# The first tile of the first expert taken from the first nine row tiles

## The chip, the cores and the metric

The kernel runs on one core of a Trainium2 chip. The metric is the device time of one execution in microseconds. The engines are PE (TensorE, matmul), PEld (its weight load), DVE (VectorE), ACT (ScalarE), POOL (GpSimd) and SP (SyncE, which only issues transfers here).

## The reference

Linear attention in eight batches feeds a mixture of eight experts that takes one expert for each token.

```python
def _attn_ref(q, k, v, g_norm):                  # (8, 8, 576, 64)
    kv = np.einsum('bhsd,bhse->bhde', k, v)
    out = np.einsum('bhsd,bhde->bhse', q, kv)
    rms = np.sqrt(np.mean(out * out, axis=-1, keepdims=True) + 1e-06)
    return (out / rms * g_norm).astype(np.float32)

def _moe_ref(x, w_gate, w_output_gate, w1, w2):  # x (4608, 512), 8 experts, F 1024
    logits = x @ w_gate
    e_idx = np.argmax(logits, axis=1)
    ...                                          # gate_w: softmax at e_idx; eom: sigmoid(x @ w_output_gate)
    for e in range(E):
        mask = e_idx == e
        h = np.maximum(x[mask] @ w1[e], 0.0)
        out[mask] = gate_w[mask, None] * eom[mask, e, None] * (h @ w2[e])
```

## The kernel before

The 4608 tokens are 36 row tiles of 128. The attention of a batch is a set of products kvps (line 563, loads kvm and rem), a transpose kvTps (581), a product with the gates mps (593), and for each row tile a product ops (642) with its evictions on ACT. The rows go to DRAM (xs, written by SP, line 1031), 16 columns of norms and scales for each row to the tables xr and xt. Row tiles are routed in four groups of 9, 7, 10 and 10 (GR). The first two groups, 16 tiles, are "early": from their rows each expert's first two tiles of 128 tokens (TA = 2) are made, so that the experts can start while the attention of the last four batches goes on. `route` is the routing of a group, in pieces: norms on DVE, the argmax, ranks by products rps (853 to 862), one-hot tiles la on DVE, ACT and POOL, a table of indices by products tblps (973). The table of the second group, the "lead", gives the indices gidx; `gather` (284) then has POOL fetch both tiles of expert 0, rows xg and norms tl each, by indirect transfers (279), and sets `issue_mark` (993), behind which SP sends the last chunk of w1.

All engines follow the order in which the code is written. `early` writes the attention of the first four batches and both routings; `late` is a generator of pieces of the later attention and routing, named `rest`, of which `early` takes four (PIECES) and `run` one behind each block of an expert. Where PE would stand idle, `constants` (531) puts products of a constant tile (cps) into its order; COLD holds their numbers.

Behind `early`, each of the two tiles is scaled by its norms on DVE (313), transposed on PE (tps, 343), split into a high and a low part (xT, by ACT 346 and DVE 347), and multiplied for f = 0 and 1 by `mm1_part` (369) in 128 columns. Weights are split likewise into whi and wlo (`split_hi`, `split_lo`, `split`). `run(0)` goes on with f = 2 to 7 over 256 columns (`mm1`, 387), with hT evicted by ACT (395) and DVE (397), and then the second layer yps (`mm2`, 423). The chunks of w2 go out on SP behind the scaling of tile 1 (a dependency in the main part). `xfree` is a pool of eight slots for kvm, qT and rows.

## Time and profile before

| | us |
|---|---|
| median of 3 runs | 585.74 (585.55 to 585.89) |
| the profiled execution: time, span | 581.15, 579.3 |
| PE busy | 555.1 (96%) |
| DVE busy | 345.7 (60%) |
| ACT busy | 285.4 (49%) |
| POOL busy | 221.2 (38%) |

The profile is of one execution. The span is what the trace shows from the first to the last instruction; the execution's own time is 1.85 us more, and the median of the runs another 4.6 us. All places below are in us from the span's start.

### The profile page before, as it was taken

How to read it: one execution, taken by the hardware profiler on the slowest of the kernel's cores; microseconds unless marked ns; L12 is line 12 of the kernel's file. 1: busy time of each engine (PE TensorE's matmuls, PEld its weight loads, DVE VectorE, ACT ScalarE, POOL GpSimd, SP SyncE). 2: the span in 40 equal slices, each digit the busy share in tenths (PEclk: the TensorE clock that was granted, in tenths of full speed). 3: DMA queues.
4: the chain of work that ended last, by engine and by line, in shares of the span. 5: the costliest groups of instructions: out<-in, count | busy, mean ns of one | idle time of the engine just before them, and what ended most of it. 6: DMA issues, size and time to landing. Idle time of an engine off the chain costs nothing.

```text
span 579.3 us, 11842 instructions
## 1 busy us (share of the span) xinstructions
PE 555.1 (96%) x4626; PEld 475.4 (82%) x4626; DVE 345.7 (60%) x634; ACT 285.4 (49%) x482; POOL 221.2 (38%) x203
## 2 busy tenths in 40 slices
PE   7998879999999999999999999999999999999995
PEld 3775668888888787988989889889897988888894
DVE  2268576565596989767586646436355463646450
ACT  1354356576567546656464434435354444535430
POOL 3342344432313252543565326235264543545202
PEclk9999999999999999999999999999999999999999
DMA  8999899797866574776855345346454645556201
GB/s 306 407 410 340 257 406 405 275 369 279 299 232 210 176 270 155 247 232 206 285 199 175 124 149 166 109 156 205 151 183 141 205 154 161 171 170 207 75 6 38
DMA packets 38586, 126.18 MB, mean 218 GB/s; under 512 B 6877, under 2 KB 8142, under 8 KB 38528
## 3 DMA queue, kind: packets, MB, share of 16 engines
q1 hardware_dynamic: 29520, 105.19, 52.4%
q0 software_dynamic: 8288, 19.82, 10.3%
q8 instruction: 38, 0.62, 0.4%
q10 hardware_dynamic: 720, 0.38, 0.2%
q14 instruction: 20, 0.16, 0.1%
HBM read 106.01 MB, written 19.91 MB: 217 GB/s over the span
## 4 chain that ended last, share of the span: by engine, by line
PE 78%; DVE 10%; DMA 5%; issue 3%; ACT 3%; POOL 1%; POOLq 0%; ACTq 0%; DVEq 0%; SPq 0%
PE hps L387 33%; PE yps L423 31%; PE ops L642 4%; PE tps L343 3%; PE kvps L563 3%; PE yps L417 3%; DVE wlo L263 2%; DMA ld<-kvm 1%; DMA wgs<-wg 1%; DMA wraw<-w 1%; ACT whi L260 1%; DVE wlo L256 1%; PE cps L538 1%; DVE hT L397 1%; DVE la L895 1%
## 5 line engine op out<-in xcount | busy, mean ns | idle before, releaser
L387 PE MATMUL hps<-xT,whi 128*128 128x256 f32 (+8 forms) x1008 | 218.0, 308 | 5.8 <-DVE hT L397 3.7
L423 PE MATMUL yps<-whi,hT 128*128 128x512 f32 (+3 forms) x592 | 199.0, 400 | 0.0
L387 PEld LDWEIGHTS hps<-xT,whi 128*128 128x128 f32 x1008 | 166.5, 190 | 12.4 <-DVE hT L397 5.2
L387 PE MATMUL hps<-xT,wlo 128*128 128x256 f32 (+8 forms) x504 | 153.2, 304 | 0.0
L423 PEld LDWEIGHTS yps<-whi,hT 128*128 128x128 f32 (+3 forms) x592 | 110.2, 186 | 24.0
L423 PE MATMUL yps<-wlo,hT 128*128 128x512 f32 (+3 forms) x296 | 116.1, 392 | 0.0
L436 POOL DMA_INDIRECT out<-y,oidx x42 | 48.7, 1160 | 173.7 <-ACT y L435 145.1
L395 ACT ACTIVATE hT<-hps 128x256 fp32r<-128x256 f32 (+8 forms) x128 | 54.9, 429 | 121.8 <-PE hps L387 116.6
L397 DVE SCALAR_TENSOR_TENSOR hT<-hps,hT 128x256 fp32r<-128x256 f32 (+9 forms) x168 | 62.9, 395 | 86.0 <-ACT hT L395 85.6
L256 DVE SCALAR_TENSOR_TENSOR wlo<-wraw,gcol,whi 128x1024 fp32r<-128x1024 f32 x62 | 84.0, 1356 | 43.5 <-ACT whi L253 41.4
L263 DVE TENSOR_TENSOR wlo<-wraw,whi 128x1024 fp32r<-128x1024 f32 x64 | 85.2, 1331 | 26.7 <-ACT whi L260 25.7
L387 PEld LDWEIGHTS hps<-xT,wlo 128*128 128x128 f32 x504 | 95.6, 190 | 0.3
L253 ACT ACTIVATE whi<-wraw,gcol 128x1024 fp32r<-128x1024 f32 x62 | 71.3, 1150 | 0.6 <-DVE wlo L263 0.6
L279 POOL DMA_INDIRECT xg<-xs,gidx x42 | 47.2, 1123 | 55.6 <-PE hps L387 36.4
L260 ACT CAST whi<-wraw 128x1024 fp32r<-128x1024 f32 x64 | 66.6, 1040 | 1.1 <-DMA wraw<-w 1.1
L279 POOL DMA_INDIRECT tl<-xt,gidx x42 | 55.3, 1316 | 28.6 <-PE hps L387 21.1
L313 POOL TENSOR_TENSOR xg<-xg,tl 128x512 f32<-128x512 f32 (+8 forms) x40 | 44.0, 1101 | 53.7 <-DMA tl<-xt,gidx 44.4
L423 PEld LDWEIGHTS yps<-wlo,hT 128*128 128x128 f32 (+3 forms) x296 | 55.3, 187 | 10.4
L435 ACT ACTIVATE y<-yps,tl 128x512 f32<-128x512 f32 (+3 forms) x37 | 25.4, 686 | 56.1 <-PE yps L423 44.1
L346 ACT CAST xT<-tps 128x512 fp32r<-128x512 f32 (+8 forms) x42 | 22.9, 546 | 41.6 <-PE tps L343 40.5
L347 DVE TENSOR_TENSOR xT<-tps,xT 128x512 fp32r<-128x512 f32 (+8 forms) x42 | 26.6, 636 | 19.5 <-ACT xT L346 19.3
L642 PE MATMUL ops<-aug,ld 64*64 64x80 f32 (+1 forms) x960 | 32.2, 244 | 1.4 <-ACT gp L673 1.3
(176 smaller groups left out, 431.2 us busy)
## 6 DMA issues: line engine op xcount, KB each, us to landing
wraw<-w SPq DMA_DIRECT2D x128, 512.0 KB, 4.6
ld<-kvm SPq DMA_DIRECT2D x32, 512.0 KB, 10.0
ld<-qT SPq DMA_DIRECT2D x18, 512.0 KB, 8.9
xs<-xrow SPq DMA_DIRECT2D x18, 512.0 KB, 4.9
ld<-rem SPq DMA_DIRECT2D x4, 512.0 KB, 5.8
xg<-xs,gidx POOLq DMA_INDIRECT x42, 4.3
tl<-xt,gidx POOLq DMA_INDIRECT x42, 4.7
out<-y,oidx POOLq DMA_INDIRECT x42, 3.3
```

Of the source, the lines that this page charges most:

```text
L253: he.activation(hi, r, AF.Copy, scale=gcol[:, 0:1])
L256: eng.scalar_tensor_tensor(out=lo, in0=r, scalar=gcol[:, 0:1], in1=hi.bitcast(F32), op0=ALU.mult, op1=ALU.subtract)
L260: he.copy(hi, r)
L263: eng.tensor_tensor(out=lo, in0=r, in1=hi.bitcast(F32), op=ALU.subtract)
L279: return nc.gpsimd.indirect_dma_start(out=o[:M, :], out_offset=None, in_=dram[0:XE] if i < E else dram, in_offset=bass.IndirectOffsetOnAxi ...
L313: return eng.tensor_tensor(out=v, in0=v, in1=f, op=ALU.mult)
L387: seq.append(nc.tensor.matmul(ps[:, :C], w[:, o:o + P], x[d][:, :C], start=(d == 0 and k == 0), stop=(d == 3 and k == 2)))
L395: nc.scalar.activation(h[:, 0:C], ps[:, :C], AF.Relu)
L397: nc.vector.scalar_tensor_tensor(out=h[:, l:l + b - a], in0=ps[:, a:b], scalar=0.0, in1=h[:, a:b].bitcast(F32), op0=ALU.max, op1=ALU.subtract)
L423: seq.append(nc.tensor.matmul(ps[:M], a, b, start=(f == 0 and n == 0), stop=(f == 7 and n == 2)))
L436: i_ = nc.gpsimd.indirect_dma_start(out=out, out_offset=bass.IndirectOffsetOnAxis(ap=oidx[i // E][:M, RUNS[i][0], t:t + 1], axis=0), in_=y ...
L642: nc.tensor.matmul(ps[c0:c0 + step_, u, p * W:(p + 1) * W], qt[g // 2][r, p, q0:q0 + step_], augs[b % 3][r, p, :], start=True, stop=True)
```

## The change

The first tile of expert 0 now takes its tokens from the first group alone, nine row tiles. Its index column gix0 is copied by ACT from the first group's table, and `gather_row(0, 0)` stands right behind that; the rows are fetched from the whole of the early rows, so the transfer waits for the last of their writes. Its norms come from a table of their own, xr0, that is zero from the tenth row tile on, is written behind the first group's norms, and is read by a gather that waits for the second group's rank products (`ranked`). If expert 0 has fewer than 128 tokens in the first group, pad0 raises its later ranks by what is missing. The second tile comes from both groups, as before.

The tile is scaled on POOL (`scale_rows`), staged in `first_tile`, and multiplied in thirds (high by high, high by low, low by high), f = 0 and 1 with the first chunk of w1 and f = 2 and 3 with the second; the low part of a weight chunk is needed only by the last third. All of f = 0 to 3 (FIRST_F) is multiplied in halves of 128 columns and lies in two tiles of PSUM. The second chunk of w1 waits for the landing of the norms of tile 0, the third for `issue_mark`, and the fourth goes out behind two loads of kvm. The pieces of the fifth batch are taken between the steps of the routing, where constants stood, and its last products come ahead of the second of its row tiles (`x != 1`). Six pieces of `rest` are taken before `run(0)`.

```diff
     def fetch(i, t, M, dram, o):
+        at = gix0 if (i, t) == (0, 0) else gidx[i // E][:M, RUNS[i][0], t:t + 1]
         return nc.gpsimd.indirect_dma_start(
             out=o[:M, :], out_offset=None, in_=dram[0:XE] if i < E else dram,
-            in_offset=bass.IndirectOffsetOnAxis(ap=gidx[i // E][:M, RUNS[i][0], t:t + 1], axis=0))
-
-
-    def gather(i, after=None):
-        for t, c0, M in tiles_of(i):
+            in_offset=bass.IndirectOffsetOnAxis(ap=at, axis=0))
+
+
+    def gather(i, after=None, only=slice(None)):
+        for t, c0, M in tiles_of(i)[only]:
...
     def stage(i, k):
+        return stage_lo(*stage_hi(i, k))
+
+    def stage_hi(i, k):
...
-        if i or not k:
+        if i or k:
             ps = ps_t.tile([P, 4, P], F32, name="tps", tag="t")
         else:
-            ps = ps_y[0].tile([P, 4, P], F32, name="tps", tag="y1")
+            ps = pair("tps")[:, 0].rearrange("p (c m) -> p c m", c=4)
...
+        return ps, hi, lo, c0, M
+
+    def stage_lo(ps, hi, lo, c0, M):
         return nc.vector.tensor_tensor(out=lo[:, :, c0:c0 + M], in0=ps[:, :, :M],
                                        in1=hi.bitcast(F32)[:, :, c0:c0 + M], op=ALU.subtract)
...
-    def mm1_part(f, part):
+    def mm1_part(f, part, thirds=(0, 1, 2)):
 
         hi, lo = ([a[:, d] for d in range(4)] for a in xT[0])
-        wh, wl = wgt[(1, f // 2)]
+        wh, wl = wgt[(1, f // 2)] if (1, f // 2) in wgt else (halved[f // 2], None)
         if 0 not in hT:
             hT[0] = rp_[0].tile([P, 8, 2 * ROWS_A], F32R, name="hT", tag="hT")
-        if f not in begun:
-            begun[f] = ps_h.tile([P, 512], F32, name="hps", tag="h")
+        if f % 2 not in begun:
+            begun[f % 2] = ps_h.tile([P, 2, ROWS_A], F32, name="hps", tag="h")
         c = slice(part * P, (part + 1) * P)
         o = (f % 2) * P
-        for n, (w, x) in enumerate(((wh, hi), (wl, hi), (wh, lo))):
+        for n in thirds:
+            w, x = ((wh, hi), (wh, lo), (wl, hi))[n]
             for d in range(4):
-                part_end[0] = nc.tensor.matmul(begun[f][:, c], w[:, d * 256 + o:d * 256 + o + P], x[d][:, c],
-                                 start=(n == 0 and d == 0), stop=(n == 2 and d == 3))
+                part_end[0] = nc.tensor.matmul(begun[f % 2][:, f // 2, c], w[:, d * 256 + o:d * 256 + o + P], x[d][:, c],
+                                               start=(n == 0 and d == 0), stop=(n == 2 and d == 3))
...
-        ps = begun.pop(f) if f in begun else ps_h.tile([P, 512], F32, name="hps", tag="h")
-        for d in range(0 if i or f > 1 else 4, 4):
+        apart = not i and f < FIRST_F
+        if apart:
+            if f % 2 == 0:
+                for g in (f, f + 1):
+                    mm1_part(g, 1)
+            ps = begun[f % 2][:, f // 2]
+        else:
+            ps = ps_h.tile([P, 512], F32, name="hps", tag="h")
+        for d in range(4 if apart else 0, 4):
...
-    for d in (xr, xt):
+    for d in (xr0, xr, xt):
         nc.gpsimd.dma_start(out=d[0:EARLY, :], in_=xtail[0:EARLY, 0, :])
+    nc.gpsimd.dma_start(out=xr0[EARLY:XE].rearrange("(m s) x -> m s x", s=EARLY)[:, GR[0]:], in_=xtail[:, GR[0]:EARLY])
...
+    cold = ps_h.tile([P, 512], F32, name="cps", tag="h")
+
+    def constants(n, after=None, ps=None):
+
+        ps = cold if ps is None else ps
...
+        if b == FIRST_B:
+            ps = ps_h.tile([P, 512], F32, name="kvps", tag="h")
+        else:
+            ps = ps_t.tile([P, 512], F32, name="kvps", tag="t")
...
+            if not gi:
+                nc.sync.dma_start(out=rows_of(xr0, g0, n), in_=xtail[:, g0:g0 + n])
...
-        if lead:
-            split_hi(0)
...
+        ranked[0] = nc.tensor.matmul(rp[:, 0:n + 1, :], triu, ohb[:, 0:n + 1, :], start=False, stop=True)
...
+        if not gi:
+            nc.scalar.activation(pad0[:, 0:1], rp[:, n, 0:1], AF.Relu, scale=-1.0, bias=cf[:, K_A0:K_A0 + 1])
+            adj.append(pad0)
...
+            if not gi:
+                nc.scalar.copy(gix0, tps[:, 0, 0:1])
+                gather_row(0, 0)
...
-            gather(0)
+            gather(0, None, slice(1, TA))
             issued.append(nc.gpsimd.memset(issue_mark, 0.0))
             vec.tensor_tensor(out=acc, in0=acc, in1=tps, op=ALU.add)
             for _ in places(0, tacc[:, 0].rearrange("p (e t) -> p e t", t=TMAX), 0, TA):
                 pass
+            first_tile()
             ea = sm.tile([P, E], F32, name="ea", bufs=1)
...
-        constants(COLD[5])
         for r in rows:
             r()
+        while early_extra:
+            send(1)
+        next(rest)
         while squares:
-            constants(COLD[2], sums())
+            constants(1, sums())
         while routing:
             advance()
-            if routing and COLD[3][at_pause[0]]:
-                constants(COLD[3][at_pause[0]], tick[0])
-        while early_extra:
-            send(1)
-        for c in w1s[:-1]:
-            wload(0, 1, c)
-        behind(wload(0, 1, w1s[-1]), issued[0])
+            if not routing:
+                break
+            k = at_pause[0]
+            if k == 1:
+                split_hi(0)
+                next(rest)
+            if k < 4:
+                constants((2, 1, 2, 2)[k], tick[0])
+            elif k == 6:
+                first_tail = behind(gather_tail(0, 0, P, xr0), ranked[0])
+                behind(wload(0, 1, w1s.pop(0)), first_tail)
+                next(rest)
+            elif k == 7:
+                constants(1, tick[0])
+            elif k == 8:
+                scale_rows(0, 0)
+                constants(1, tick[0])
+        for f, n in ((0, 0), (0, 1), (1, 0), (1, 1), (0, 2), (1, 2), (2, 0), (3, 0), (2, 1), (3, 1)):
+            mm1_part(f, 0, (n,))
+        behind(wload(0, 1, w1s.pop(0)), issued[0])
         assert len(xfree) > 2
         load([late_loads.pop(0) for _ in range(2)], xfree)
-        for k in range(PIECES):
-            next(rest)
-        constants(COLD[4], tick[0])
+        wload(0, 1, w1s.pop(0))
+
+    def first_tile():
+
+        head = stage_hi(0, 0)
+        next(rest)
+        split_hi(1)
+        stage_lo(*head)
+        split_lo(0)
...
-                    if run_out(lim):
+                    if (b > FIRST_B or x != 1) and run_out(lim):
...
+            if i == 0 and f in (3, 5, 6, 7):
+                split(0, 2, (3, 5, 6, 7).index(f))
             if f % 2:
-                split(i, 2, f // 2)
+                if i:
+                    split(i, 2, f // 2)
...
-        staged = []
-        for k in range(TA):
-            scaled_ = scale_heads(xg[(0, k)], tails[(0, k)], nc.vector)
-            if not k:
-                split_lo(0)
-            else:
-                for c in range(4):
-                    tc.add_manual_dep(wload(0, 2, c).ins, scaled_.ins.name,
-                                      mybir.DependencyInfo(mybir.DependencyClass.Sync, mybir.DependencyReason.DATA),
-                                      reason="order of the transfers")
-                late_open[0] = True
-                load(late_loads, xfree, 1)
-            staged.append(stage(0, k))
-            for f in range(2):
-                mm1_part(f, k)
-            if not k:
-                split_hi(1)
+        scaled_ = scale_heads(xg[(0, 1)], tails[(0, 1)], nc.vector)
+        for c in range(4):
+            tc.add_manual_dep(wload(0, 2, c).ins, scaled_.ins.name,
+                              mybir.DependencyInfo(mybir.DependencyClass.Sync, mybir.DependencyReason.DATA),
+                              reason="order of the transfers")
+        late_open[0] = True
+        load(late_loads, xfree, 1)
         split_lo(1)
+        stage(0, 1)
+        for f in (2, 3):
+            mm1_part(f, 0, (2,))
+        next(rest)
+        next(rest)
```

POOL, from the last la tile of the second group to the mark (xg: rows, tl: norms, gidx0 and gix0: indices). Before:

```order
L895 TENSOR_SCALAR la_960<-ni_64,rlon_940 128x128
L279 DMA xg_983<-xs,gidx0_74 128x512
L279 DMA tl_985<-xr,gidx0_74 128x16
L279 DMA xg_987<-xs,gidx0_74 128x512
L279 DMA tl_989<-xr,gidx0_74 128x16
L993 MEMSET issue_mark_137 128x1
```

With the change:

```order
L283 DMA xg_883<-xs,gix0_78 128x512
L283 DMA tl_949<-xr0,gix0_78 128x16
L922 TENSOR_SCALAR la_982<-ni_64,rlon_974 128x128
L922 TENSOR_SCALAR la_992<-ni_64,rlon_974 128x128
L317 TENSOR_TENSOR xg_883<-xg_883,tl_949 128x512
L283 DMA xg_1014<-xs,gidx0_74 128x512
L283 DMA tl_1016<-xr,gidx0_74 128x16
L1023 MEMSET issue_mark_143 128x1
```

The first pair of gathers stands ahead of two la tiles, a scaling has come in between the pairs, and the mark follows the second pair as before.

SP, the chunks of w1 that follow the early loads, up to the first chunk of w2 (xs: the write of rows 16 and 17). Before:

```order
L217 DMA wraw_1012<-w1 128x1024
L217 DMA wraw_1014<-w1 128x1024
L217 DMA wraw_1016<-w1 128x1024
L528 DMA ld_1018<-kvm 128x1024
L528 DMA ld_1020<-kvm 128x1024
L1031 DMA xs<-xrow_1042 128x1024
L217 DMA wraw_1152<-w2 128x1024
```

With the change:

```order
L220 DMA wraw_951<-w1 128x1024
L220 DMA wraw_1102<-w1 128x1024
L549 DMA ld_1104<-kvm 128x1024
L549 DMA ld_1106<-kvm 128x1024
L220 DMA wraw_1108<-w1 128x1024
L220 DMA wraw_1115<-w2 128x1024
```

The third chunk of w1, wraw_1102, is the one behind the mark; it was the fourth, wraw_1016. The write of rows is no longer among them, and the fourth chunk stands behind the two loads.

PE, the second kvps pair of the sixth batch (kvps x16: 8 products for each of two loads of kvm) among the blocks of expert 0. Before, the end of f = 5 and the start of f = 6:

```order
L387 MATMUL hps<-xT,whi 128x256 x2
L387 MATMUL hps<-xT,wlo 128x256
L563 MATMUL kvps<-ld 64x64 x16
L387 MATMUL hps<-xT,whi 128x256 x2
L387 MATMUL hps<-xT,wlo 128x256
```

With the change, from mps (the second halves of f = 0 and 1 stand ahead) to the start of f = 4:

```order
L616 MATMUL mps<-gw,kvT 64x16 x8
L586 MATMUL kvps<-ld 64x64 x16
L380 MATMUL hps<-xT,whi 128x128 x8
L380 MATMUL hps<-xT,wlo 128x128 x4
L380 MATMUL hps<-xT,whi 128x128 x8
L380 MATMUL hps<-xT,wlo 128x128 x4
L665 MATMUL ops<-aug_128,ld 64x80 x16
L586 MATMUL kvps<-ld 64x64 x16
L405 MATMUL hps<-xT,whi 128x256 x2
L405 MATMUL hps<-xT,wlo 128x256
```

The lower kvps x16 is that pair; it has moved from between f = 5 and f = 6 to ahead of f = 4, and the ops ahead of it is that of row tile 18.

## Rows read from the trace of the kernel before

**Rows 1.** Busy PE, PEld, DVE, ACT, POOL; PEclk, DMA share, GB/s.
```profile
72.50:75.50 3.00, 2.90 (x37) 2.69 (x36) 2.24 (x4) 1.48 (x3) 0.44 (x1) 1.00 1.02 407
...
95.00:150.00 55.00, 55.00 (x683) 47.81 (x681) 31.16 (x44) 34.55 (x63) 19.15 (x17) 1.00 0.87 314
```

**Rows 2.** PE's timeline: start, us, work [idle before], expert 0's blocks.
```profile
82.69 0.50 PE L387 MATMUL hps<-xT,whi 128*128 128x256 f32 x2 [0.68 <-DVE hT L397]
...
84.31 0.79 PE L642 MATMUL ops<-aug,ld 64*64 64x80 f32 x32
...
86.55 0.51 PE L387 MATMUL hps<-xT,whi 128*128 128x256 f32 x2 [1.45 <-DVE hT L397]
...
88.17 1.15 PE L563 MATMUL kvps<-ld 128*64 128x64 f32 x32
...
93.82 0.50 PE L423 MATMUL yps<-whi,hT 128*128 128x512 f32 x1
```

**Rows 3.** The same timeline, before and at expert 0's first products.
```profile
54.42 2.75 PE L538 MATMUL cps<-ones 128*128 128x512 bf16 x11 [0.17 <-DVE ry L730]
...
57.99 0.19 PE L862 MATMUL rps<-ohb,triu 128*128 128x64 bf16 x1
...
60.07 0.87 PE L973 MATMUL tblps<-rrc,la 128*128 128x16 bf16 x14 [1.03 <-DVE rrc L938]
...
67.80 0.66 PE L369 MATMUL hps<-xT,whi 128*128 128x128 f32 x4 [0.67 <-ACT xT L346]
...
70.53 0.63 PE L343 MATMUL tps<-ident,xg 128*128 128x128 f32 x4
```

**Rows 4.** POOL's timeline: gathers, the mark and a scaling.
```profile
61.43 1.10 POOL L279 DMA_INDIRECT xg<-xs,gidx  x1 [0.84 <-DVE tacc L994]
...
64.10 0.95 POOL L279 DMA_INDIRECT xg<-xs,gidx  x1 [0.30 <-issue]
...
66.30 0.11 POOL L993 MEMSET issue_mark<- 128x1 f32 x1
...
82.76 1.97 POOL L313 TENSOR_TENSOR xg<-xg,tl 128x512 f32<-128x512 f32 x1 [0.62 <-DMA tl<-xr,gidx]
...
93.52 1.05 POOL L313 TENSOR_TENSOR xg<-xg,tl 128x512 f32<-128x512 f32 x1 [4.86 <-DMA tl<-xr,gidx]
```

**Rows 5.** The chain that ended last, in time, 62 to 67 us.
```profile
62.83 2.81 DMA tl<-xr,gidx
...
65.72 0.70 DVE xg L313
```

**Rows 6.** SP's timeline, issues of transfers, 49 to 77 us.
```profile
50.12 3.31 SPq L1031 DMA_DIRECT2D xs<-xrow  x2
...
66.44 0.33 SPq L217 DMA_DIRECT2D wraw<-w  x1
...
66.82 0.90 SPq L528 DMA_DIRECT2D ld<-kvm  x2
...
67.83 0.37 SPq L1031 DMA_DIRECT2D xs<-xrow  x1
...
74.28 2.22 SPq L528 DMA_DIRECT2D ld<-kvm  x2
```

**Rows 7.** Issues at 53.1, 66.44, 66.82, 67.83, 76.17: KB, us to landing.
```profile
xs<-xrow SPq DMA_DIRECT2D x1, 512.0 KB, 3.8
...
wraw<-w SPq DMA_DIRECT2D x1, 512.0 KB, 3.6
...
ld<-kvm SPq DMA_DIRECT2D x1, 512.0 KB, 5.6
...
xs<-xrow SPq DMA_DIRECT2D x1, 512.0 KB, 8.3
...
ld<-kvm SPq DMA_DIRECT2D x1, 512.0 KB, 11.9
```

**Rows 8.** PE's timeline at the start of the kernel.
```profile
1.03 4.51 PE L538 MATMUL cps<-ones 128*128 128x512 bf16 x11 [1.03 <-DVE ones L158]
```

More of the change, by code (lines that the diff above doesn't have):

```diff
@@ L472, in body @@
     adj = []
+    pad0 = c1.tile([P, E], BF16, name="pad0")
+    nc.vector.memset(pad0, 0.0)
     triu = c1.tile([P, P], BF16, name="triu")
@@ L1113, in early @@
             if b == FIRST_B - 2:
-                constants(COLD[5])
+                constants(COLD[3])
             more()
```

23 lines of the change are left out of this document (10 added, 13 removed).

## The prediction

> **What bounds the kernel now.** I read the windows first. From 95 to 150 us PE is busy for all 55.00 us [rows 1], and the waits that follow are small, so from the first second-layer product of expert 0 (yps, 93.82 us [rows 2]) the end of the kernel keeps a fixed distance: what the change gives or takes is what it does to that start, once work that was moved across it is counted. Then I read PE's timeline up to there. Until 67.80 us PE has nothing to multiply for expert 0 and runs constants, among them eleven in a row at 54.42 [rows 3]. The chain of that stretch is a chain of latencies: routing of the second group on DVE, its table on PE (60.07, 0.87 us [rows 3]), then on POOL four gathers and the mark, 61.43 to 66.41 [rows 4]. The tail of tile 0 lands 2.81 us after its issue [rows 5], at 65.64, and only then can tile 0 be scaled and transposed.
>
> Last I read SP's timeline with the landings, and it is what I rest on. SP stands still before the fourth chunk of w1 until the mark is set; the load goes out at 66.44 [rows 6], and behind it a stream of twelve transfers of 512 KB that the rest of the stage lives on: that chunk, two of kvm, one write of rows, four of w2, two of qT, two of kvm. The first lands 3.6 us after issue (70.04), the second at 72.42 (66.82 + 5.6), the fourth at 76.13 (67.83 + 8.3) [rows 6, 7]. The twelfth goes out at 76.17 (the end of the row at 74.28, less one issue of 0.33 us) and lands 11.9 us later, at 88.07. The product that needs it, the second kvps pair of the sixth batch (an early piece of the later attention), stands at 88.17 [rows 2, 6, 7]. So in this stage PE and the transfers arrive together: there is no slack in the transfers.
>
> **The change part by part.**
>
> *Tile 0 early.* Its gather no longer waits for the second group. Its index is known after the table of the first group, which is ready before 54.42, but the row gather must still wait for the last rows: issued at 53.1 (50.12 + 3.31 - 0.33), landed 3.8 us later, 56.9 [rows 6, 7]. Gather of rows 56.9 to 58.0. The gather of norms waits for the rank product of the second group (57.99 + 0.19 [rows 3]), goes out at 58.25 and lands at 61.06 by the 2.81 us of [rows 5]; two la tiles that stand behind it on POOL end before that. Scaling moves from DVE to POOL: 1.05 us is what the same operation takes there at 93.52, 1.97 us at 82.76 [rows 4]; I take 1.1, since DVE has only small operations then. So PE transposes at 62.25 and has products from about 63.6, 4.2 us earlier than 67.80.
>
> *PE's own work.* Constants between the first rank product and the first transpose go from 33 to 15: 18 fewer at 0.25 us (2.75 / 11 [rows 3]), 4.5 us, all in places where PE waited anyway. Against that f = 2 and 3 are now also multiplied in halves of 128 columns. A block of 24 such products takes 2.73 us (67.80 to 70.53 [rows 3]) against 1.62 us for 12 of 256 columns (82.69 to 84.31 [rows 2]): 2 x 1.11 = 2.2 us more PE work. Following PE through the new order at 0.114 us for a product of a half (2.73 / 24; four thirds 1.8, two with wlo 0.9, four of chunk 1 1.8, transposes 0.65, two more thirds 0.9, a row of ops 0.7, f = 0 and 1's second halves 2.7, mps and the first kvps pair 1.5, f = 2 and 3's second halves 2.7) PE would stand at the ops of tile 18 at 77.8 and at the second kvps pair at 78.6. The extra 2.2 us are paid here, in time that PE then spends waiting; without that wait they would count in full.
>
> *The transfers.* POOL's chain is now scale, gather, gather, mark: 62.15, 62.3 to 63.4, 63.7 to 64.65, mark at 64.75. SP lets the third chunk of w1 go at 64.8, 1.65 us earlier than 66.44. (The second chunk waits for the tail, 61.2, and lands at 64.8 by the 3.6 us; its use at 66.5 comes after it.) The stream behind the mark again has twelve transfers up to the second kvps pair: chunk 3, two of kvm, chunk 4, four of w2, two of qT, two of kvm. The write of rows falls behind it. First landing 68.4, second 2.38 later (as before, 72.42 - 70.04). The next two took 1.86 each in before, with the write among them; at the steady rate of 407 GB/s [rows 1] 512 KB take 1.29. I take 1.29 for both, the bounds being 1.86 (startup is slow whatever is moved) and, for all three, 1.29. Then 11.94 us from the fourth to the twelfth, as before (76.13 to 88.07), which holds the next tile's two gathers. Sum 64.8 + 3.6 + 2.38 + 2.58 + 11.94 = 85.3; bounds 84.2 and 86.4. So the data come 2.8 us earlier.
>
> *The order in which they are asked for.* The batch work now runs two pieces ahead: the second kvps pair stands in front of f = 4, not in front of f = 6. Behind its last chunk's landing there used to be 5.75 us to the first yps (88.07 to 93.82). Now there are half the pair 0.54, four blocks of 1.62, two ops of 0.71, the remainder's kvps 0.61 and a transpose 0.2: 9.25, with 0.05 to start 9.3. Of these one ops and the transpose, 0.86, stood behind the first yps before. So the tail grows by 9.3 - 5.75 - 0.86 = 2.7 us. This is where the gain goes: 4 us earlier products are followed by a wait of some 3.5 us for qT at ops (the ninth transfer, near 81) and of some 3 us for kvm. DVE and ACT have caught up by then; their evictions of f = 3 and 4 end before PE asks.
>
> *The rest.* The second row of norms (one more SP issue of some 0.33 us, well ahead of 50.12), two small transfers at the start and pad0 lie beside other work: nothing, at most 0.3 us if the write were late.
>
> Net: -2.8 + 2.7 = -0.1 us. The profiled execution shows a span of 579.3 us and a time of 581.15; the median of the runs is 585.74. I add the difference to the median: **585.6 us, no measurable change** (0.2%, 1.2 us, is what a measurement of this kernel can tell from none).
>
> **The rivals.**
>
> *Faster.* The stream is quicker than in before: no write in it, and it starts on queues that a lone chunk has kept running. All steps at 1.29 give 84.2 (-1.2 us); if the gathers too cost nothing beside it (11.94 becomes 8 x 1.29 = 10.3), 82.6, and -2.8 us: 583.0. The far bound is no wait at all, PE at the second pair at 78.6, where DVE's evictions still hold f = 5 until 83: about -5 us, 580.8. For it: the transfers ran at 407 GB/s a little later. Against it: the first three steps of the stream did not, and nothing shows that the write was the reason. Time of this rival 584.0 (half of the way).
>
> *Slower: the clock.* PE has waits of 3 us and more in 77.8 to 85, filled with one ops and half a pair, where constants used to stand in earlier gaps. [...] The longest wait in this stage before, 1.45 us ahead of 86.55, did not lower the granted clock: the block behind it takes 1.62 us (86.55 to 88.17) like the one at 82.69 [rows 2]. The waits I expect are twice as long. It decides from where the waits are longer than any that this trace shows at full clock: +1.8 on 585.6, 587.4, and 588.2 with the upper bound of the stream.
> [...]
>
> *Not what it says.* The mark is not earlier: POOL's scale takes 1.97 us and the tail lands late, so that the stream starts at 66 or after. It costs up to 1.65 us: 587.2.
> In the trace the scaling is 0.70 us on DVE [rows 5] against 1.05 on POOL; the move itself costs 0.35 to 0.4, which the sum above has, and with 1.97 it costs 0.9 more, 586.5.
> [...]
>
> **How the numbers follow.** No change, 0.45; faster, 0.27; the clock or a late stream, 0.20; the mark not earlier, 0.08. So faster 0.27, same 0.45, slower 0.28. The range reaches into the faster rival beyond its middle and to the clock with a slow stream: 583.6 to 588.2. The forecast's own range is 584.5 to 586.8.
>
> **What would show it.** In the profile after: first transposes of tile 0 near 62.3 and hps near 63.6; the mark near 64.75 and the next w1 load 0.05 us behind it; waits of PE for qT and kvm between 77 and 86, several us long, at ops and kvps; the last kvm of that pair landing near 85.3; the first yps near 94.6. If PE shows no wait for kvm there, the step on the transfers is wrong and the kernel is faster. If the granted clock falls below 1.00 between 78 and 92, the clock rival holds. If the mark is at 66, the last one.

## The result

The changed kernel takes 591.77 us, median of four executions (590.43 to 593.62), against 585.82 us before (585.55 to 586.44, four executions beside it): a ratio of 1.0102, 95% interval 1.0074 to 1.0131. It is slower by 6 us, 1%. The prediction was 585.6 us, no measurable change, with a range of 583.6 to 588.2. The result is outside that range, in a direction that the prediction gave 0.28. Executions of one kernel differ here by several us, in part with the granted clock of TensorE (the kernel before on one chip: 583.37 us at a mean clock of 0.999, 593.84 at 0.977), so the mean clock of a profiled execution is given where it matters: 0.967 in the changed kernel's (span 591.5 us), 0.999 in that of before (span 579.3). Ratios leave out executions more than 1.5% above the fastest of their kernel, medians do not.

Where the time goes is on the profile page after, in two of the forty slices' lines, PE's busy tenths and its granted clock in tenths (a slice is 14.8 us):

```profile
PE   7998899999999998999999999999999999999995
...
PEclk9999656999999998999999999999999999999999
```

The fifth to the seventh slice, 59 to 104 us, have a clock of 0.6, 0.5 and 0.6 with PE busy eight tenths or more. Windows of one microsecond in that stretch (length, then busy PE, PEld, DVE, ACT, POOL with their instructions, granted clock, DMA share, GB/s):

```profile
60.00:61.00 1.00, 0.67 (x11) 0.46 (x11) 1.00 (x4) 0.00 (x0) 0.96 (x3) 1.00 0.54 201
61.00:62.00 1.00, 0.42 (x9) 0.23 (x6) 0.46 (x3) 0.00 (x0) 0.56 (x2) 1.00 0.04 4
62.00:63.00 1.00, 0.10 (x1) 0.10 (x2) 0.97 (x4) 0.00 (x0) 0.85 (x2) 1.00 0.44 61
...
64.00:65.00 1.00, 0.94 (x10) 0.80 (x6) 0.79 (x2) 0.18 (x1) 0.70 (x2) 0.54 0.67 172
...
92.00:93.00 1.00, 0.97 (x14) 0.72 (x10) 0.65 (x2) 0.00 (x0) 0.66 (x1) 0.50 0.22 74
...
97.00:98.00 1.00, 1.00 (x32) 1.00 (x32) 0.64 (x3) 0.38 (x1) 0.00 (x0) 0.50 0.35 124
98.00:99.00 1.00, 1.00 (x14) 0.83 (x10) 0.46 (x1) 0.68 (x2) 0.00 (x0) 0.90 0.07 20
```

PE has little to do ahead of 63 (0.67, 0.42 and 0.10 of the first windows shown), the clock falls near 64.1, and it is back only near 98.2. In between PE is busy nearly all the time (0.94 to 1.00 of the microseconds shown up to 98), at a granted clock of 0.50 from 65 to 98. PE's timeline, with the idle time before an instruction and what ended it in brackets:

```profile
62.90 0.66 PE L350 MATMUL tps<-ident,xg 128*128 128x128 f32 x4 [1.22 <-POOL xg L317]
...
64.23 3.67 PE L380 MATMUL hps<-xT,whi 128*128 128x128 f32 x16
...
90.11 1.35 PE L665 MATMUL ops<-aug,ld 64*64 64x80 f32 x32
...
93.20 0.92 PE L586 MATMUL kvps<-ld 128*64 128x64 f32 x12 [0.23 <-issue]
94.05 0.80 PE L405 MATMUL hps<-xT,whi 128*128 128x256 f32 x2
...
104.44 0.48 PE L441 MATMUL yps<-whi,hT 128*128 128x512 f32 x1
```

The first sixteen products of tile 0 take 3.67 us, 0.229 each, twice the 0.114 of [rows 3]. The waits for qT (ahead of the ops at 90.11) and for kvm that the prediction saw at 77.8 to 85 are not there: PE comes to those places so late that the data have long arrived; 0.23 us ahead of the row at 93.20 is all, and the profile names no transfer for it. The first yps is at 104.44 instead of 93.82 [rows 2], 10.6 us later. What the span has more, 12.2 us, is that and 1.6 us behind it, part of which is a second, short fall of the clock (last section). These two profiles are a quick execution of before (581.15 us) and the longest of the four after (593.62), 12.5 us apart; the medians are 6.0 apart.

The early first tile itself came nearly as foreseen. POOL in the profile after:

```profile
57.72 1.10 POOL L283 DMA_INDIRECT xg<-xs,gix  x1 [4.82 <-ACT gp L696]
59.12 0.98 POOL L283 DMA_INDIRECT tl<-xr,gix  x1 [0.30 <-issue]
...
61.80 1.04 POOL L317 TENSOR_TENSOR xg<-xg,tl 128x512 f32<-128x512 f32 x1 [0.44 <-DMA tl<-xr,gix]
...
65.28 0.13 POOL L1023 MEMSET issue_mark<- 128x1 f32 x1
```

The rows of tile 0 are fetched at 57.72 (foreseen 56.9; in before all gathers start at 61.43 [rows 4]), its norms at 59.12 (58.25), the scaling takes 1.04 us (1.1), and the mark is set at 65.28 (64.75, before 66.30). Transposes at 62.90 (62.25) and products at 64.23 (63.6) are 3.6 us earlier than in before.

### The profile page after: what moved, and what is told of

Same layout as the page of the kernel before. It is cut to its first block, busy times and chain, and to the rows that moved or that the text cites. A ratio compares the mean times of both kernels' runs of the same rounds, so it can differ in the third digit from the quotient of the medians.

```text
span 591.5 us, 11871 instructions
## 1 busy us (share of the span) xinstructions
PE 570.4 (96%) x4635; PEld 492.3 (83%) x4635; DVE 343.8 (58%) x634; ACT 285.4 (48%) x484; POOL 219.7 (37%) x206
## 4 chain that ended last, share of the span: by engine, by line
PE 84%; DVE 5%; DMA 4%; issue 3%; ACT 2%; POOL 1%; POOLq 0%; ACTq 0%; DVEq 0%
PE hps L405 33%; PE yps L441 32%; PE ops L665 5%; PE hps L380 4%; PE kvps L586 3%; PE tps L350 3%; PE yps L435 2%; DVE wlo L266 2%; DMA ld<-kvm 1%; DMA wgs<-wg 1%; PE cps L558 1%; ACT whi L263 1%; DVE wlo L259 1%; DMA xs<-xrow 1%; DVE hT L415 1%
## 5 line engine op out<-in xcount | busy, mean ns | idle before, releaser
L454 POOL DMA_INDIRECT out<-y,oidx x42 | 46.6, 1110 | 175.4 <-ACT y L453 147.9
L266 DVE TENSOR_TENSOR wlo<-wraw,whi 128x1024 fp32r<-128x1024 f32 x64 | 83.9, 1311 | 25.5 <-ACT whi L263 21.8
L317 POOL TENSOR_TENSOR xg<-xg,tl 128x512 f32<-128x512 f32 (+8 forms) x41 | 45.7, 1116 | 54.5 <-DMA tl<-xt,gidx 43.9
L441 PEld LDWEIGHTS yps<-wlo,hT 128*128 128x128 f32 (+3 forms) x296 | 55.2, 186 | 10.3
L283 POOL DMA_INDIRECT tl<-xt,gidx x41 | 51.0, 1245 | 26.4 <-PE hps L405 18.5
L665 PE MATMUL ops<-aug,ld 64*64 64x80 f32 (+1 forms) x960 | 33.7, 255 | 1.3 <-ACT gp L696 0.6
```

Of the source, the lines that this page charges most:

```text
L266: eng.tensor_tensor(out=lo, in0=r, in1=hi.bitcast(F32), op=ALU.subtract)
L283: return nc.gpsimd.indirect_dma_start(out=o[:M, :], out_offset=None, in_=dram[0:XE] if i < E else dram, in_offset=bass.IndirectOffsetOnAxi ...
L317: return eng.tensor_tensor(out=v, in0=v, in1=f, op=ALU.mult)
L441: seq.append(nc.tensor.matmul(ps[:M], a, b, start=(f == 0 and n == 0), stop=(f == 7 and n == 2)))
L454: i_ = nc.gpsimd.indirect_dma_start(out=out, out_offset=bass.IndirectOffsetOnAxis(ap=oidx[i // E][:M, RUNS[i][0], t:t + 1], axis=0), in_=y ...
L665: nc.tensor.matmul(ps[c0:c0 + step_, u, p * W:(p + 1) * W], qt[g // 2][r, p, q0:q0 + step_], augs[b % 3][r, p, :], start=True, stop=True)
```

## The experiments

Two theories were set against each other. Theory 1: the constants that the change took away had kept the clock up, and without them it falls. Theory 2: the new products of tile 0, thin (128 columns) and in one long piece, are what it falls under. All ratios are to the kernel before, run beside it on the same chip. The kernels were run on several chips, and the kernel before itself took 582 to 586 us on them, so only ratios are compared across chips. Even those move by 0.8 points for one and the same kernel: the version of the last experiment has 0.9979 on one chip and 0.9903 on another.

**The two kernels again, unchanged.** Does the clock fall in the kernel before, too, and is the changed kernel's loss there on another chip?

> The kernel before, unchanged, to see the granted clock of its timed executions, since its profiled one (581.15 us) lies 4.6 under the median (585.74). Both theories expect a ratio of 1.000. If the clock also falls in some of its executions, their mean clock is under 0.999 and their time 4 to 6 us above the profiled one's; if not, all are at 0.999 and the 4.6 us have another cause.

> The changed kernel, unchanged, beside the next three and the kernel before on the same chip. Both theories expect the low stretch of the clock near 64 to 98 again, a first yps at 103 to 105, and a ratio of 1.008 to 1.013.

The kernel before against itself: 581.92 us median of ten, ratio 0.999 (0.997 to 1.0011). Its profiled execution, 584.16 us at a mean clock of 0.985, has a fall the first profile did not show:

```profile
69.00:70.00 1.00, 1.00 (x9) 1.00 (x9) 0.00 (x0) 0.00 (x0) 0.00 (x0) 0.73 1.09 221
83.00:84.00 1.00, 1.00 (x21) 0.78 (x21) 0.93 (x3) 0.69 (x2) 0.58 (x1) 0.94 1.06 414
```

The clock fell near 69.5, within the first products of tile 0, and was back near 83.1. So the kernel before can have such a stretch, of 14 us here; the mean clocks of its ten executions are 0.983 to 0.998. The 581.15 us of the first profile was an execution without it (0.999). The changed kernel on the second chip: 592.8 us, ratio 1.0106 (1.0077 to 1.0135), mean clocks of 0.959 to 0.972 in all ten, so that by these the long stretch is in every execution.

**Constants in the gaps ahead of the first transposes.**

```diff
             elif k == 7:
-                constants(1, tick[0])
+                constants(3, tick[0])
             elif k == 8:
                 scale_rows(0, 0)
-                constants(1, tick[0])
+                constants(3, tick[0])
...
     def first_tile():
+        constants(5)
         head = stage_hi(0, 0)
```

> The changed kernel with nine more constants on PE: three instead of one at each of the two places behind the second group's rank products, and five between the table of indices and the first transposes, where PE idled 0.51 and 1.22 us with little else in 57 to 63. Theory 1 (the constants that the change took away let the clock fall at 64.5, and it stays at half until 98): the clock stays at 1.00 from 57 to 95, the products of a half take 0.114 us instead of 0.229, the first yps comes at 94 to 96 instead of 104.4, and the time is 584.5 to 587.5. Theory 2 (the new products themselves, thin and with no break, are what the clock falls under): the clock falls at about the same place, first yps 104 to 105, 591 to 593 us.

585.54 us, ratio 1.0039 (1.0017 to 1.0062). The expected times start from a kernel before at 585.8 us; as ratios they are 0.998 to 1.003 for theory 1 and 1.009 to 1.012 for theory 2. So this is nearer to theory 1, somewhat above it, and the first yps, at 98.61, is later than its 94 to 96. In the profile the clock stays at 1.00 from 57 to 82 (66 to 67 is shown below), and so the waits that the prediction described come out:

```profile
65.02 2.28 PE L380 MATMUL hps<-xT,whi 128*128 128x128 f32 x16
...
82.90 1.35 PE L665 MATMUL ops<-aug,ld 64*64 64x80 f32 x32 [3.35 <-DMA ld<-qT]
85.35 1.12 PE L586 MATMUL kvps<-ld 128*64 128x64 f32 x16 [1.10 <-DMA ld<-kvm]
87.24 1.12 PE L586 MATMUL kvps<-ld 128*64 128x64 f32 x16 [0.76 <-DMA ld<-kvm]
```

3.35 us for qT (foreseen some 3.5), then 1.10 and 0.76 for kvm (foreseen some 3). And the clock falls there instead:

```profile
66.00:67.00 1.00, 1.00 (x11) 1.00 (x11) 0.96 (x3) 1.00 (x1) 0.20 (x2) 1.00 0.58 182
...
81.00:82.00 1.00, 0.00 (x0) 0.00 (x0) 0.93 (x8) 0.00 (x0) 0.93 (x1) 1.00 1.01 414
82.00:83.00 1.00, 0.10 (x4) 0.13 (x8) 0.93 (x6) 0.00 (x0) 0.02 (x1) 0.50 1.04 426
...
92.00:93.00 1.00, 1.00 (x21) 0.89 (x14) 0.70 (x2) 0.49 (x2) 0.00 (x0) 0.88 1.05 426
```

PE stood idle ahead of 82.90, the clock is at 0.50 from 82 and back near 92.2. That is the place of the prediction's slower rival; the loss by the ratios of this run and of the next, 0.39 and 0.54% or 2 to 3 us, is somewhat more than its 1.8. The ops behind the wait of 3.35 us take 1.35 us; in the variant with 256 columns further down, the ops behind a wait of 2.10 us take 0.78. The same kernel a second time, beside the next two variants:

> The gap variant once more, unchanged, beside the next three. In the runs of the variants built on it the clock fell near 66, a microsecond or two into the thin products, although PE had stood idle little before. Theory 1 (the removed constants alone let the clock fall): no long low stretch, mean clock 0.98 to 0.99, ratio 1.003 to 1.005. Theory 2 (a run of thin products can bring it down by itself): low from 66 to 93 in part of the executions, mean clock 0.97 there, median ratio 1.005 to 1.015 if they are the most.

Ratio 1.0054 (1.0034 to 1.0074), mean clocks 0.984 to 0.990, by which none has the long stretch; in the profiled one the clock is down from 79.6 to 89.9 and, by windows of 3 us, from 216.2 to 219.6.

**Constants taken out of the kernel before** (seventeen by the trace, 71 to 54, one less than its expectation says).

```diff
-COLD = (1, 10, 2, (3, 3, 3, 2, 0, 0, 2, 2, 0, 2), 5, 3)
+COLD = (1, 10, 2, (2, 1, 1, 0, 0, 0, 1, 0, 0, 0), 0, 3)
```

> The kernel before with 18 constants fewer between the first group's table and the first transposes, 14 instead of 32 or so, and nothing else changed. Theory 1: the granted clock falls to 0.50 between 58 and 68 and stays low for a stretch of 15 to 35 us; each 1 us at the low clock costs up to 0.5 us, so 590 to 600 us. Theory 2 (constants there do nothing): clock 1.00, 585.8 us within 1.

Half of it came. The clock does fall in the gap that the constants left:

```profile
61.00:62.00 1.00, 0.00 (x0) 0.10 (x1) 0.90 (x5) 0.42 (x2) 0.32 (x1) 0.81 0.95 377
...
68.00:69.00 1.00, 1.00 (x32) 0.93 (x34) 0.76 (x2) 0.59 (x2) 0.86 (x2) 0.78 0.71 217
```

But it is back near 68.4, behind the kvps and ops that stand there and ahead of the first transposes, and PE had waits in that place anyway. Three of the ten executions took 586.39 to 587.01 us at mean clocks of 0.974 to 0.977, lower than any of the unchanged kernel's ten; of the 31 executions of the kernel before beside them two took 587.27 and 587.66 us, at 0.979. Median 581.95 us, ratio 0.9988 (0.9952 to 1.0024). Without them the clock can fall there in the old order too, and that cost nothing measurable in the median; so the missing constants don't explain by themselves why the stretch of the changed kernel is so long and dear.

**What ends the low stretch.** Sixteen constants behind the thirds of tile 0 (line `stage(0, 1)`), and, in another kernel, f = 2 and 3 multiplied in 256 columns as before.

```diff
         split_lo(1)
+        constants(16, None, ps_y[0].tile([P, DM], F32, name="cps", tag="y1"))
         stage(0, 1)
```

> The changed kernel with 16 constants put behind the first ten thirds of tile 0 (near 72.8, when the clock has been low for 8 us). It asks what ends the low stretch. Theory 1a (wide bf16 products raise the granted clock again, as at the start of the kernel, the thin fp32 ones do not): they take 0.41 us each until the clock returns near 77 and less from there; the products from 79 on take half as long as in the changed kernel, first yps 98 to 100 and 586 to 588 us. Rival (it comes back only by itself, near 98): the constants cost 16 x 0.41 = 6.6 us, first yps near 109, 596 to 598 us.

Granted clock, row of the constants and first yps:

```profile
64.00:65.00 1.00, 1.00 (x10) 0.87 (x6) 0.83 (x2) 0.84 (x4) 0.70 (x1) 0.50 0.66 172
...
76.00:77.00 1.00, 1.00 (x4) 0.30 (x2) 0.00 (x0) 0.00 (x0) 0.00 (x0) 0.50 1.01 414
...
78.00:79.00 1.00, 1.00 (x9) 0.69 (x7) 0.00 (x0) 0.00 (x0) 0.00 (x0) 1.00 1.04 426
```

```profile
72.79 5.97 PE L558 MATMUL cps<-ones 128*128 128x512 bf16 x16
...
98.43 0.48 PE L441 MATMUL yps<-whi,hT 128*128 128x512 f32 x1
```

The constants take 5.97 us, and the clock is back near 77.5 with them instead of near 98. (The start of the kernel, which theory 1a names, does not show such a rise: its eleven constants take 4.51 us [rows 8], but the granted clock on record is 1.00 in every microsecond from 1 to 6, in the profiles before and after.) Six microseconds of products that compute nothing cost less than they give back: the first yps comes at 98.43 instead of 104.44 (expected 98 to 100). 586.55 us, ratio 1.0054 (1.0025 to 1.0083), against the 1.0102 and 1.0106 of the changed kernel on other chips.

```diff
-FIRST_F = 4
+FIRST_F = 2
...
-        for f, n in ((0, 0), (0, 1), (1, 0), (1, 1), (0, 2), (1, 2), (2, 0), (3, 0), (2, 1), (3, 1)):
+        for f, n in ((0, 0), (0, 1), (1, 0), (1, 1), (0, 2), (1, 2)):
...
-        for f in (2, 3):
-            mm1_part(f, 0, (2,))
```

> The changed kernel, without more constants, with f = 2 and 3 multiplied in 256 columns as before instead of in halves. It asks whether the long low stretch (34 us) is that of the thin products. Theory 1b (under the thin fp32 products the clock stays low, under products of 256 columns it rises again, as it did near 92 in the gap variant and near 82 in the kernel before): the clock falls near 64.5 again and is back by 84 to 92 instead of 98; first yps 99 to 102, ratio 1.004 to 1.009. Rival (it comes back at a time of its own): back at 98 again, ratio 1.009 to 1.013.

585.47 us, ratio 0.9987 (0.9945 to 1.0029), against 1.0106 of the changed kernel beside it on the same chip: the whole loss is gone with that one edit, which also takes the 2.2 us of additional products off PE. In the profiled execution (mean clock 0.982) the clock falls near 62 all the same, but it is back much sooner than I expected:

```profile
68.59 1.91 PE L380 MATMUL hps<-xT,wlo 128*128 128x128 f32 x8
70.30 1.07 PE L350 MATMUL tps<-ident,xg 128*128 128x128 f32 x4
71.31 1.32 PE L665 MATMUL ops<-aug,ld 64*64 64x80 f32 x32
72.56 0.44 PE L604 MATMUL kvTps<-ident,kvc 128*128 128x128 f32 x2
```

The products of tile 0 end at 70.3, transposes and ops follow, and the kvTps at 72.56 and all behind it up to 86 run at full clock (1.00 in every microsecond from 73 to 86), and the clock has come back before the first product of 256 columns. (At 86.1, behind waits for kvm, it falls once more, to 89.5.) So it is not the 256 columns that bring it back, as theory 1b had it. What the runs show is which work stood ahead of each rise: transposes and ops in one piece here, constants in the last one, products of 256 columns in the changed kernel (from 94.05) and in the gap variant (from 88.29); and that in the profiles it stayed low while the halves of f = 0 to 3 went on with single ops, kvps and transposes between them. The stretches of 24 to 34 us are all of kernels with FIRST_F = 4; with FIRST_F = 2 there is one of 10 us here and one of 20.5 in the version without more constants further down. So the length of the stretch goes with the long run of halves; that they are also what the clock falls under is not shown by this.

**The order and the waits.** What is left of the loss when the gaps are filled: the order, or the clock in the waits for qT and kvm? Both variants are built on the gap kernel: four pieces of `rest` ahead of `run(0)` instead of six (the order of before behind f = 3), and constants in those waits.

```diff
         for f in (2, 3):
             mm1_part(f, 0, (2,))
-        next(rest)
-        next(rest)
```

> The gap variant (nine more constants ahead of the first transposes) with four pieces of the later attention ahead of the experts' blocks as before instead of six: the ops of row tile 18 stand behind f = 4 again and the second kvps pair behind f = 5. Theory 1 (with the first fall of the clock cured, what is left of the loss is the order: PE stands idle 5.2 us at qT and kvm and the clock falls there): the last kvm still lands near 87, behind it 5.75 us to the first yps as before, so 92 to 93.5 instead of 99 or so; the idle time ahead of ops falls from 3.35 to under 2 us, the clock stays at 1.00 or falls for less than 5 us; ratio 0.996 to 1.001. Rival (the order costs nothing, the transfers are simply late): the waits for qT and kvm stay as long and the ratio stays near 1.004.

```diff
-            run(i, lambda n: next(rest, None))
+            run(i, lambda n: (constants(12 if n == 2 else 4, None, ps_y[0].tile([P, DM], F32, name="cps", tag="y1"))
+                              if i == 0 and n in (2, 3) else None, next(rest, None)))
```

> The gap variant with twelve more constants ahead of the ops of row tile 18 and four ahead of the second kvps pair, where PE waits 3.35 us for qT and 1.1 us for kvm. They take 3.0 and 1.0 us of that idle time. Theory 1: the clock stays at 1.00 from 57 to 100, the blocks behind the pair take 1.62 us each instead of 2.5, first yps about 96.5, ratio 1.000 to 1.002 (0.3 to 0.4% better than the gap variant's 1.004). Rival (the clock in that wait costs nothing that is not waited out anyway): as the gap variant, 1.004.

Neither question was answered. Of four executions of each, three had the long low stretch (587.79 to 588.48 us, and 592.23 to 594.62, at mean clocks of 0.971 to 0.977) and one not (579.07 and 584.70, at 0.998 and 0.993), too few for a ratio. Theory 1 alone was thereby in doubt, since the nine constants were back in the gaps of both. The next variant was to tell: the gap kernel with a constant behind each third of tile 0.

```diff
+        breaker = pair("cps")[:, 0]
         for f, n in ((0, 0), (0, 1), (1, 0), (1, 1), (0, 2), (1, 2), (2, 0), (3, 0), (2, 1), (3, 1)):
             mm1_part(f, 0, (n,))
+            constants(1, None, breaker)
```

> The gap variant with one constant behind each of the ten thirds of tile 0 (ten constants, 2.5 us, of which the wait of 3.35 us for qT takes up all). Theory 2: the thin products no longer run in one piece, the clock does not fall at 66 or is back before 75, mean clock 0.98 or more, ratio 1.002 to 1.005, with none of the executions at 0.97. Theory 1: nothing that the gap variant doesn't show but a shorter wait for qT.

584.51 us, ratio 1.0031 (1.0008 to 1.0054), against 1.0054 of the gap kernel beside it, with mean clocks of 0.988 to 0.993. But on that chip the gap kernel itself had no long stretch, so this does not tell the theories apart; the ten constants may only have shortened the wait for qT (0.20 us ahead of that ops in the profile, 3.25 in that of the gap kernel beside it). The two variants once more:

> The gap variant with four pieces ahead of the blocks, as before, unchanged from the first time: ops of row tile 18 behind f = 4, second kvps pair behind f = 5. In the one execution of the first time without the long low stretch it took 579.07 us where the kernel before took 584 to 587. If the order is what is left of the loss: ratio 0.993 to 0.998 in executions without that stretch, against 1.005 of the gap variant. If the order is nothing: 1.003 to 1.006.

> The gap variant with sixteen constants in PE's waits for qT and kvm, order as in the changed kernel, unchanged from the first time. If the half clock in and behind those waits (81 to 92) is what is left of the loss: 1.000 to 1.002, first yps 95 to 96 and the clock at 1.00 from 57 to 97. If it is the order: 1.004 to 1.006 still.

The profile of the first shows the fall of theory 2, with no long gap ahead of it:

```profile
66.00:67.00 1.00, 0.92 (x9) 0.89 (x8) 0.93 (x5) 1.00 (x2) 0.00 (x0) 1.00 0.53 119
67.00:68.00 1.00, 1.00 (x12) 1.00 (x10) 0.93 (x3) 0.11 (x1) 0.00 (x0) 0.95 0.89 283
68.00:69.00 1.00, 1.00 (x7) 1.00 (x7) 1.00 (x1) 0.00 (x0) 0.00 (x0) 0.50 1.01 328
```

PE was busy for 0.78 or more of each microsecond from 60 on, and the clock fell near 68, among the products of tile 0. Five of the twelve executions of either variant have the long stretch (586.97 to 590.41 us, and 590.51 to 593.29, at 0.968 to 0.980). The order of before: 581.2 us, ratio 0.9925 (0.9888 to 0.9961), faster than before for all that. The filled waits: 586.56 us, ratio 0.9998 (0.9961 to 1.0035). Their executions without the stretch are 578.79 to 581.27 and 583.61 to 587.02 us, some 4 us apart (medians 580.3 and 584.4). That speaks for the order as a term of the sign that was foreseen and not smaller than the 2.7 us; the sixteen constants, by which the two variants differ too, are not separated from it.

The profiled execution of the filled waits holds the clock at 1.00 from 57 to 97 and nearly so throughout, and so shows the changed kernel as the prediction drew it. The line of its page on the granted clock, in the same forty slices as above, and PE's rows:

```profile
PEclk9999999999999999999999999999999999999999
...
64.15 2.60 PE L380 MATMUL hps<-xT,whi 128*128 128x128 f32 x16
...
78.87 2.76 PE L558 MATMUL cps<-ones 128*128 128x512 bf16 x12
...
84.91 0.69 PE L586 MATMUL kvps<-ld 128*64 128x64 f32 x16 [0.70 <-DMA ld<-kvm]
...
94.10 0.48 PE L441 MATMUL yps<-whi,hT 128*128 128x512 f32 x1
...
99.62 0.78 PE L665 MATMUL ops<-aug,ld 64*64 64x80 f32 x32 [2.07 <-ACT gp L696]
```

Data at 84.9 (foreseen 85.3), first yps at 94.10 (foreseen 94.6), and by the ratio no difference to the kernel before (foreseen none). At like clocks there is none either: two executions of this variant at a mean clock of 0.999 took 583.61 and 584.01 us, four of the kernel before beside it at 0.999 took 583.37 to 584.92. The row at 99.62 is a wait that the prediction did not have: 2.07 us for ACT's evictions, behind the first yps, where [rows 1] show no idle time before.

**A version that keeps the early tile and leaves the two parts out that cost.** The early first tile, f = 2 and 3 in 256 columns and the order of before, first without more constants, then with constants in the gaps (3, 3 and 5 ahead of the transposes, 9 behind the thirds, 5 ahead of the ops of row tile 18).

```diff
-FIRST_F = 4
+FIRST_F = 2
...
         split_lo(1)
         stage(0, 1)
-        for f in (2, 3):
-            mm1_part(f, 0, (2,))
-        next(rest)
-        next(rest)
```

> The changed kernel with f = 2 and 3 in 256 columns and with the order of before behind it (four pieces ahead of the blocks, the second kvps pair behind f = 5), without more constants: the early first tile without the two parts that are suspected. It separates the order from the thin products: with f = 2 and 3 in 256 columns alone the ratio was 0.999. If the order costs 2.7 us (the second kvps pair with four blocks behind it instead of two), first yps 92 to 95 and 0.993 to 0.997; if it costs nothing, 0.999 again.

To that, the edit of the gap kernel and:

```diff
         split_lo(1)
+        constants(9, None, ps_y[0].tile([P, DM], F32, name="cps", tag="y1"))
         stage(0, 1)
...
-            run(i, lambda n: next(rest, None))
+            run(i, lambda n: (constants(5, None, ps_y[0].tile([P, DM], F32, name="cps", tag="y1"))
+                              if i == 0 and n == 4 else None, next(rest, None)))
```

> The same with constants: three, three and five in the gaps ahead of the first transposes, nine behind the thirds of tile 0, where PE now waits for tile 1, and five ahead of the ops that waits for qT. Theory 1 and 2 alike: the clock stays at 1.00 from 57 to 95 in most executions, first yps 91 to 92.5, ratio 0.988 to 0.994, that is faster than both kernels. If the clock falls all the same, 0.997 to 1.003.

Plain: 581.47 us, ratio 0.9988 (0.9959 to 1.0018), mean clocks of 0.973 to 0.985. By its expectation the ratio speaks for an order that costs nothing, and the first yps, at 94.50, for one that costs 2.7 us; with the clock down from 61.6 to 82.1 in its profile the two are not told apart, and the early tile brings nothing. With constants: 580.21 us, ratio 0.9979 (0.9952 to 1.0005), mean clocks of 0.992 to 0.999 in eleven of twelve. Again, on the chip of the two repetitions, and beside it the kernel before with fifteen more constants in its own gaps between 67 and 87, to see whether the constants alone are the gain:

> The variant with the early first tile, f = 2 and 3 in 256 columns, the order of before and constants in every gap, once more. If its gain is real: 0.994 to 0.999 again, first yps 91 to 92.

```diff
             staged.append(stage(0, k))
+            constants(2)
...
-            run(i, lambda n: next(rest, None))
+            run(i, lambda n: i == 0 and n == 2 and constants(4) or (next(rest, None), i == 0 and n in (3, 4) and constants((2, 5)[n - 3])))
```

> The kernel before with fifteen more constants in PE's idle gaps between 67 and 87 (two behind each of the two transposes, four ahead of mps, two behind the first kvps pair, five ahead of f = 5) and nothing else changed. If the variant's gain comes from a steadier clock alone, this one has it too: 0.994 to 0.998, mean clock 0.995 or more. If it comes from the earlier first tile, this one stays at 0.999 to 1.002 and the variant is ahead of it by 0.2 to 0.4%.

The version: 580.92 us, ratio 0.9903 (0.9869 to 0.9937), faster than the kernel before. Its PE timeline:

```profile
86.48 0.69 PE L586 MATMUL kvps<-ld 128*64 128x64 f32 x16 [0.38 <-DMA ld<-kvm]
...
91.66 0.50 PE L441 MATMUL yps<-whi,hT 128*128 128x512 f32 x1
```

The pair stands behind f = 5 at 86.48, and the first yps comes at 91.66, 2.2 us before that of [rows 2]. The kernel before with more constants: 585.65 us, ratio 1.0004 (0.9974 to 1.0034), and its profiled execution, at a mean clock of 0.989, still has falls at 60.7, 67.5 and 81.2. Constants alone are not the gain there; but since they did not make the clock steadier (0.983 to 0.998 in the twelve), this does not measure what a steady clock alone would bring. The executions at like clocks tell more. On the first of the two chips eight of the version at 0.997 and above took 578.77 to 580.51 us, five of the kernel before 580.38 to 583.22 (medians 580.1 and 582.1); on the second all six of the version took 580.21 to 581.91, the six of the kernel before at 0.998 and above 583.37 to 584.92. So some 2 to 3 us of the gain, an estimate from these, are there without a difference of the clock. What the rest is, the runs don't divide.

## Why the prediction was wrong

*The step that failed* is the path of PE through the new order, which was followed "at 0.114 us for a product of a half", that is at full clock, with the 2.2 us of the halves "paid here, in time that PE then spends waiting". In the profile after, the clock is at half from 64.1 to 98.2 and such a product takes 0.229 us. From the first products to the end of the second halves of f = 3 PE takes 25.9 us (64.23 to 90.11) against 14.7 at full clock in the filled variant (64.15 to 78.87), 11.2 more. PE then has no waits left in which to pay, and at the first yps 10.3 us are still there (104.44 against 94.10; 94.6 was foreseen).

*The early first tile* was right: gathers, scaling, transposes and products within 0.9 us of what was foreseen, and the mark 0.5 us late. The transfers were right in the filled variant, where the last kvm of the pair is used at 84.91 (85.3 was foreseen); in the gap variant it is at 87.24, with the first products 0.9 us later than there. The sign that the prediction gave for a mistake here, no wait for kvm and therefore a faster kernel, came out false: the wait is missing in the changed kernel because PE is late, not because the data are early.

*The constants* were costed at nothing: eighteen fewer were set down as 4.5 us "all in places where PE waited anyway". Whether they also kept PE's clock up was not asked. How much of the fall is theirs stays open. With nine of them back the profiled clock stays at 1.00 until 82, and the ratio is 1.0039 and 1.0054 instead of 1.0106; but that is on other chips, and the difference is no larger than the 0.8 points by which one kernel's ratio moved between two chips. With the same nine in place the long stretch came in half of the executions of two variants on two more chips, and seventeen fewer in the old order cost nothing measurable.

*f = 2 and 3 in halves* are the part without which the loss is not there: 0.9987 beside 1.0106 on the same chip. Their 2.2 us more are the price at full clock only.

*The order* was right in sign, as far as the runs show it: 2.7 us were foreseen for the longer tail, and the variant with four pieces is some 4 us faster than the one with six, both without the low stretch, though they differ by sixteen constants too. In the profiles the tail itself, from the use of the last kvm to the first yps, is 9.2 us with six pieces (84.91 to 94.10; 9.3 was foreseen) and 5.2 with four (86.48 to 91.66; 5.75 in before).

*The slower rival* was right that the clock can fall in this stage, but had the wrong place and far too small a price. It asked where PE would wait newly, and found the waits for DMA at 77.8 to 85; the clock had fallen more than 13 us ahead of that. No run shows the 1.8 us at which it priced the low clock; what the runs showed is half speed for all that PE does until the clock is back, 10.3 us at the first yps in the profile after, and a loss of 2 to 3 us by the ratios of the gap kernel, which was low from 82 to 92.2 in its profile.

*What the number was added to* was weak as well. The profiled execution of before was one without a fall of the clock, and its median 4.6 us above it; I carried the difference along without asking what it was. It need not be the clock: executions of the kernel before at a mean clock of 0.998 and above took 580.4 to 582.1 us on two chips and 583.4 to 584.9 on two others.

Some sums of the prediction are off by little: the terms of PE's path add up to about 77.3, not 77.8, and the times of the faster and the clock rival by 0.1 to 0.3 us. Nothing above depends on it.

## What to carry to other kernels

Idle time of PE that is filled with products that compute nothing need not be free room (sixteen such products took 5.97 us here, and the first yps came 6.0 us earlier with them): before taking such products out, ask for the granted clock of that stretch, and price the work behind it at the low clock until a row shows the clock back (0.229 us instead of 0.114 for a product of a half here, 1.35 instead of 0.78 for a row of ops). A rearrangement that splits the same products into narrower ones is to be read for both, the time they take (2.73 us instead of 1.62 for a block here) and what the clock does under them (low from 64.1 to 98.2 in the changed kernel, from 62.2 to 72.5 with f = 2 and 3 in 256 columns). And a forecast for a kernel whose executions differ by the clock needs the clock of several executions, not of the one that was profiled.

## What the runs showed of the hardware

The granted clock stayed at half for 34 us (64.1 to 98.2 in the profile after), most of them with PE busy without a break, and in one execution it fell with PE busy for 0.78 or more of every microsecond of the eight before (the variant with four pieces, at 68). What work would and would not bring it back was shown only by what stood ahead of the rises, and the same program fell or did not fall in one place: the filled variant was at 0.70 from 66 to 67 and at 0.50 behind it in one profiled execution, and at 1.00 from 57 to 97 in another, on another chip. Counted by mean clocks of 0.980 and below, the gap kernel had two such executions in sixteen on two chips, one of them the profiled one, whose clock stays at 1.00 from 57 to 82; two variants of it with the same products on PE up to 70 us had sixteen in thirty-two on two others. Why is open.

The profile after has a second fall, from 224.5 to 227.9, behind a wait for DVE:

```profile
223.91 0.50 PE L405 MATMUL hps<-xT,whi 128*128 128x256 f32 x2 [1.96 <-DVE hT L415]
...
226.19 0.63 PE L405 MATMUL hps<-xT,whi 128*128 128x256 f32 x2
```

PE waits 1.96 us ahead of 223.91, and the blocks behind it run at half clock (0.50 from 225 to 227), some 1.5 us lost (an estimate from three products that take 0.64 us there, 224.91 to 225.55, and 0.36 ahead of the wait, 220.72 to 221.08). The filled variant and the version above had none there.
